# Three early experts, with their rows fetched ahead of the last routing, in an attention, FFN and mixture-of-experts kernel on Trainium2

## The chip, the cores and the metric

The kernel runs on one core of one Trainium2 chip, as one program and one launch. The metric is the device time of one execution in microseconds (us). The kernel before takes 1385.56 us, the median of three runs (1384.43 to 1387.48).

## The reference

Three stages, in float32. Attention: 4 batches of 8 heads, 576 positions of 64 values, where each query keeps its 32 best keys. FFN: 2304 tokens of 512 values, 2048 hidden values, squared ReLU. Then a mixture of experts, which the change concerns:

```python
logits = x @ w_gate
noise_scale = np.log1p(np.exp(x @ w_noise))
noisy_logits = logits + noise_scale * noise
top2 = np.argpartition(-noisy_logits, 2, axis=1)[:, :2]
...
for e in range(E):                      # 8 experts, 512 -> 1024 -> 512
    for k in range(2):
        mask = top2[:, k] == e
        h = np.maximum(x[mask] @ w1[e], 0.0)
        out[mask] += top2_w[mask, k, None] * (h @ w2[e])
```

## The kernel before, in words

Tokens go in 18 tiles of 128, in six chunks of three tiles (`CHUNKS`, L23). While attention works on later chunks, the FFN of finished ones runs as filler: `step` (L656) takes pieces from a list `background`, and, between them, pieces of the routing of a finished chunk (`route`, L177). The order in which each engine gets its instructions is made by a planner when the program is built: it goes by priority (mostly program order) and by a simulated time line; each engine then runs its list in order and waits on semaphores.

`route` turns the chunk's rows, computes the gates, counts how many tokens each expert has had so far (`base`) and scatters each token's row twice, by indirect DMA on POOL, into `xs` in DRAM, where every expert has its own slots (L259). The scatters are told to be independent of each other. A later read of `xs` waits for the scatters that stand ahead of it in program order.

`fetch(e, parts)` (L556) is a generator. For each tile of 128 slots it loads the rows from `xs` into `mr` (three buffers, issued on SyncE, L563), turns them with four TensorE transposes into a PSUM bank called `ph` (L566), writes a high and a low half into `xe` (ACT L570, DVE L571), and has POOL compute the gates into `info` (L548 to L554; `info` has two buffers). It yields after each tile, and at the end yields `xe` and `info`.

`expert(e, parts, ahead)` (L578) first gathers the present output rows into `cur` (POOL, L588), then makes 8 steps f. A step loads 512 KB of weights (`raww`, three buffers, L608), splits them into `wi` and `wo` (ACT L612, DVE L613; two buffers each), multiplies (`ph`, L619 to L621, two banks, 12 matmuls for each part), makes `ht` (ACT L625, DVE L626), and then does the second product of the step before (`second`, L596: `acc`, L600 to L602, three matmuls for each tile). From the second step on it advances the generator `ahead`, which fetches the next expert's rows. At the end DVE makes `y` (L640, three buffers) and POOL scatters it into `out` (L641). Slots are in two parts: 0 to 383 and 384 to 639 (`PARTS`, L77).

`EARLY` is 2: experts 0 and 1 work on the first part of their slots alone, behind the last FFN chunk and beside the last chunk's routing. So that the last chunk's tokens don't come into these slots, `ffn` raises `base` to 384 for the early experts (L313 to L316). When five of six chunks are routed, expert 0's rows are fetched (L827); expert 1's are fetched by expert 0 as `ahead`, and expert 1 waits with `once_routed` for the last routing before it fetches those of expert 2 (L831 to L840). Then come experts 2 to 7 with both parts, and then the second parts of experts 0 and 1, with their weights loaded again (`order`, L828; loop, L881).

`queued` (L166) stamps a matmul or transpose, and TensorE gets the stamped ones in program order. Stamped are all of the experts' matmuls, the transposes of `fetch`, and the TensorE work of the last routing; the FFN's are not.

Of the kernel before, what the change touches and what calls it, by code (L numbers as in the profile page):

```python
# [8 lines left out]
F32 = mybir.dt.float32  # L9
F32R = mybir.dt.float32r  # L10
# [7 lines left out]
P = 128  # L18
# [15 lines left out]
ROUTE_WAIT = 30  # L34
LAST_WAIT = 8
EXPERT_WAIT = 60
EARLY = 2
SOON = 300
FILL_LATER = 350
CONVERT_LATER = 200  # L40
# [15 lines left out]
def attention_ffn_moe(ctx: ExitStack, tc: tile.TileContext, q, k, v, w_ffn, w_route, noise, w_exp, out,  # L56
# [5 lines left out]
    NT, DM = out.shape  # L62
# [5 lines left out]
    NC = DM // P  # L68
# [8 lines left out]
    PARTS = [(0, 384), (384, CAP - 384)]  # L77
# [85 lines left out]
        nc.sync.dma_start(wsc[f][:, which], sp.bitcast(F32))  # L163


    def queued(inst):  # L166
        tc.stamp_issue_order_token(inst.ins, "experts")

    def evacuate(accs):
        xrs = []  # L170
# [104 lines left out]
    def ffn(t0, nt, xT):  # L275
# [37 lines left out]
        if t0 + nt == NTT:  # L313
            for e in range(EARLY):
                nc.vector.tensor_scalar(base[:, e:e + 1], base[:, e:e + 1], float(e * NT + PARTS[0][1]), None,
# [228 lines left out]
    def place(parts, t):  # L544
        return next((i, t * P - o) for i, (o, n) in enumerate(parts) if o <= t * P < o + n)

    def gate(gi, xr, e):
        nc.gpsimd.tensor_scalar(gi[:, 0:1], xr[:, DM + 2:DM + 3], float(e), xr[:, DM:DM + 1],  # L548
                                op0=ALU.is_equal, op1=ALU.mult)
        nc.gpsimd.tensor_scalar(gi[:, 1:2], xr[:, DM + 2:DM + 3], float(e), None, op0=ALU.is_equal)  # L550
        nc.gpsimd.tensor_scalar(gi[:, 1:2], gi[:, 1:2], -1.0, 1.0, op0=ALU.mult, op1=ALU.add)
        nc.gpsimd.tensor_tensor(gi[:, 1:2], gi[:, 1:2], xr[:, DM + 1:DM + 2], op=ALU.mult)
        nc.gpsimd.tensor_tensor(gi[:, 2:3], gi[:, 0:1], gi[:, 1:2], op=ALU.add)
        nc.gpsimd.tensor_copy(gi[:, 3:4].bitcast(I32), xr[:, DM + 3:DM + 4].bitcast(I32))  # L554

    def fetch(e, parts):  # L556

        xe = [mpool.tile([P, 2, NC, n], F32R, name=f"xe{o}") for o, n in parts]
        t0, t1 = parts[0][0] // P, sum(parts[-1]) // P
        info = mpool.tile([P, CAPT, 4], F32, name="info")  # L560
        for t in range(t0, t1):
            xr = mpool.tile([P, ROW], F32, name="mr", bufs=3)
            nc.sync.dma_start(xr, xs[e * NT + t * P:e * NT + (t + 1) * P, :])  # L563
            pt = ps_m.tile([P, DM], F32, name="ph")
            for c in range(NC):
                queued(nc.tensor.transpose(pt[:, c * P:(c + 1) * P], xr[:, c * P:(c + 1) * P], ident))  # L566
            i, off = place(parts, t)
            hi, lo = xe[i][:, 0, :, off:off + P], xe[i][:, 1, :, off:off + P]
            pv = pt.rearrange("p (c s) -> p c s", c=NC)
            nc.scalar.activation(hi, pv, AF.Copy)  # L570
            nc.vector.tensor_tensor(lo, pv, hi.bitcast(F32), op=ALU.subtract)  # L571
            gate(info[:, t, :], xr, e)
            yield None
        yield xe, info
# [3 lines left out]
    def expert(e, parts, ahead):  # L578
# [17 lines left out]
        def second(f, wo, hs):  # L596
            for t in tiles_:
                i, off = place(parts, t)
                sl = slice(off, off + P)
                queued(nc.tensor.matmul(acc[t], hs[i][:, 0, sl], wo[:, 0, :], start=(f == 0), stop=False))  # L600
                queued(nc.tensor.matmul(acc[t], hs[i][:, 0, sl], wo[:, 1, :], start=False, stop=False))  # L601
                queued(nc.tensor.matmul(acc[t], hs[i][:, 1, sl], wo[:, 0, :], start=False, stop=(f == NFE - 1)))  # L602
                yield True, 0.5
# [42 lines left out]
    found = []  # L646
# [9 lines left out]
    def step(n):  # L656

        state["due"] += n
        at = tc.cur_priority
        tc.cur_priority = at + FILL_LATER  # L660
        while state["due"] > 0 and (background or routing):
            cost = 1.0
            if routing and state["safe"] and routing[0][1] <= 0:
                try:
                    routing[0][1] = next(routing[0][0])
                    cost = 0.5
                except StopIteration:
                    routing.pop(0)
                    state["routed"] += 1
                    continue  # L670
            elif background:
                try:
                    state["safe"], cost = next(background[0][0])
                    background[0][1] -= cost
                except StopIteration:
                    state["safe"] = True
                    state["chunk"] += 1
                    background.pop(0)
                    continue
            state["due"] -= cost  # L680
            if routing:
                routing[0][1] -= cost
        if not background and not routing:
            state["due"] = 0.0
        tc.cur_priority = at
# [36 lines left out]
    for b in range(1, B):  # L722
        last = max(n for n, u in enumerate(units) if u[0] == b - 1)
# [97 lines left out]
    mpool = wctx.enter_context(tc.tile_pool(name="mpool", bufs=2))  # L821
    ps_m = wctx.enter_context(tc.tile_pool(name="ps_m", bufs=2, space=PSUM))
    after.append(ps_m)
    step(EXPERT_WAIT)
    while state["routed"] < len(chunks) - 1:
        step(1)
    found.append(list(fetch(0, PARTS[:1]))[-1])  # L827
    order = [(e, PARTS) for e in range(EARLY, E)] + [(e, PARTS[1:]) for e in range(EARLY)]  # L828
    last = fetch(*order[0])

    def once_routed(rows):  # L831
        while state["routed"] < len(chunks):
            yield None
        yield None
        yield None
        yield from rows

    for e in range(EARLY):
        ahead = fetch(e + 1, PARTS[:1]) if e + 1 < EARLY else once_routed(last)
        background.append([expert(e, PARTS[:1], ahead), 0])  # L840
    step(10 ** 6)

# [35 lines left out]
    for x in last:  # L878
        if x is not None:
            found.append(x)  # L880
    for i, (e, parts) in enumerate(order):  # L881
        ahead = fetch(*order[i + 1]) if i + 1 < E else iter(())
        for _ in expert(e, parts, ahead):
            pass
# [80 lines left out]
def build(shapes):  # L965
    import concourse.bacc as bacc

    nc = bacc.Bacc("TRN2", target_bir_lowering=False, num_devices=1)
    args = []
    for name, (shape, dt) in shapes.items():  # L970
        ap = nc.dram_tensor(name, shape, dt, kind="ExternalInput").ap()
        args.append(ap.bitcast(U32) if dt == mybir.dt.uint64 else ap)
    args.append(nc.dram_tensor("out", (2304, 512), F32, kind="ExternalOutput").ap())
    B, H, S, _ = SHAPE
    n_rows = B * H * (S // P) + B * H // 2
    with tile.TileContext(nc, schedule_with_timeline_sim=True) as tc, \
            tc.tile_pool(name="kpool", bufs=1) as kpool:
        keep = kpool.tile([P, n_rows, 4], F32, name="keep")
        attention_ffn_moe(tc, *args, keep=keep)
    return nc  # L980
# [61 lines left out]
```

## Time and profile before

| | before |
|---|---|
| median of three runs | 1385.56 us |
| the profiled execution, its own time | 1387.6 us |
| its span, first to last instruction | 1385.9 us |
| TensorE (PE) busy | 1246.5 us, 90% |
| TensorE weight loads (PEld) busy | 1084.5 us, 78% |
| VectorE (DVE), ScalarE (ACT), GpSimd (POOL) busy | 63%, 61%, 56% |
| mean granted TensorE clock | 0.962 |
| moved by DMA | 257.45 MB, mean 186 GB/s |

Busy time is a share of the whole span, over stages with different limits. Attention ends at about 760 us, the last FFN chunk at 878, and from there to the end the experts run. A group's mean time of a matmul is longer than the distance from one to the next, as matmuls are pipelined: for the pace one reads the starts.

### The profile page before, as it was taken

What the parts mean: (1) busy time and instruction counts of PE and PEld (TensorE: products, weight loads), DVE (VectorE), ACT (ScalarE), POOL (GpSimd) and SP (SyncE); (2) the same over time, 40 slices, a digit from 0 to 9 for tenths busy, and PEclk for the clock granted to TensorE, in tenths of its full rate; (3) what the DMA queues carried; (4) which work ended last, traced back from release to release, by engine and by line L of the source; (5) the groups of instructions that cost most, each with busy time, mean ns of one, the idle gap of its engine ahead of it and who ended that gap; (6) DMA issues with size and microseconds to landing.
All of it is one profiled execution on the core that took longest, in us unless ns stands there. A gap on an engine that the chain in (4) does not pass through costs nothing.

```text
span 1385.9 us, 25688 instructions
## 1 busy us (share of the span) xinstructions
PE 1246.5 (90%) x7937; PEld 1084.5 (78%) x7937; DVE 877.1 (63%) x4514; ACT 851.7 (61%) x1837; POOL 773.2 (56%) x1239
## 2 busy tenths in 40 slices
PE   3666689889999999899999999969999999999997
PEld 2555578768887887788888888759988898888986
DVE  7999979897767888988797001335444434444354
ACT  6888788888788888978796334524333233232343
POOL 6868999867776767777575424424413315041132
PEclk9786699999999999999999999989999999999999
DMA  9996688724764455275325767446534434343344
GB/s 333 352 345 228 208 309 296 261 91 153 251 209 142 143 178 191 62 237 183 130 92 176 270 224 263 146 139 198 163 125 127 142 117 149 111 150 118 119 155 144
DMA packets 85235, 257.45 MB, mean 186 GB/s; under 512 B 10716, under 2 KB 10844, under 8 KB 85088
## 3 DMA queue, kind: packets, MB, share of 16 engines
q1 hardware_dynamic: 75808, 227.32, 49.6%
q0 software_dynamic: 9280, 28.40, 5.7%
q8 instruction: 65, 1.06, 0.3%
q14 instruction: 82, 0.67, 0.1%
HBM read 205.71 MB, written 52.06 MB: 186 GB/s over the span
## 4 chain that ended last, share of the span: by engine, by line
PE 39%; issue 23%; DMA 9%; POOL 9%; DVE 9%; ACT 7%; POOLq 0%; SPq 0%; ACTq 0%; DVEq 0%
PE pa L491 5%; PE acc L282 4%; PE acc L283 4%; PE ps L371 4%; PE acc L284 4%; PE pf L296 3%; PE pf L298 3%; PE pf L297 3%; PE pa L454 3%; DMA out<-y,info 3%; DVE w L388 2%; POOL cur L588 2%; DMA mr<-xs 2%; DMA raw<-in_ffn 2%; DVE m L384 2%
## 5 line engine op out<-in xcount | busy, mean ns | idle before, releaser
L384 DVE MAX8 m<-sb 128x8 f32<-128x115 f32 (+1 forms) x720 | 191.7, 266 | 69.4 <-ACT sb L373 64.3
L442 POOL TENSOR_TENSOR sb<-sb,w 128x576 f32<-128x576 f32 x144 | 205.7, 1430 | 45.7 <-ACT w L441 44.4
L641 POOL DMA_INDIRECT out<-y,info x40 | 46.0, 1150 | 269.8 <-DVE y L640 252.6
L388 DVE MATCH_REPLACE8 w<-m,sb 128x115 f32<-128x115 f32 (+1 forms) x720 | 188.0, 264 | 0.0
L371 PE MATMUL ps<-K,qt 128*128 128x288 f32 (+2 forms) x640 | 134.1, 339 | 47.4 <-ACT sb L373 27.1
L619 PE MATMUL ph<-xe,wi 128*128 128x384 f32 (+1 forms) x512 | 163.4, 319 | 8.8 <-DVE ht L626 8.8
L620 PE MATMUL ph<-xe,wi 128*128 128x384 f32 (+1 forms) x512 | 158.7, 310 | 0.0
L621 PE MATMUL ph<-xe,wi 128*128 128x384 f32 (+1 forms) x512 | 158.4, 309 | 0.1
L371 PEld LDWEIGHTS ps<-K,qt 128*128 128x128 f32 x640 | 106.5, 210 | 64.6 <-ACT sb L373 36.1
L625 ACT ACTIVATE ht<-ph 128x384 fp32r<-128x384 f32 (+1 forms) x128 | 55.9, 437 | 148.4 <-PE ph L621 141.8
L612 ACT ACTIVATE wo<-raww 128x512 fp32r<-128x512 f32 x80 | 50.4, 631 | 143.7 <-PE acc L602 143.7
L306 POOL TENSOR_TENSOR gt<-r,gt 128x384 fp32r<-128x384 f32 x96 | 97.8, 1020 | 69.0 <-ACT gt L305 53.4
L443 ACT ACTIVATE sb<-sb,keep 128x576 f32<-128x576 f32 x144 | 112.2, 779 | 27.6 <-POOL sb L442 26.6
L626 DVE SCALAR_TENSOR_TENSOR ht<-ph,ht 128x384 fp32r<-128x384 f32 (+1 forms) x128 | 62.7, 490 | 101.9 <-ACT ht L625 100.8
L602 PE MATMUL acc<-wo,ht 128*128 128x512 f32 x320 | 126.6, 396 | 0.1
L600 PE MATMUL acc<-wo,ht 128*128 128x512 f32 x320 | 126.7, 396 | 0.0
L601 PE MATMUL acc<-wo,ht 128*128 128x512 f32 x320 | 126.3, 395 | 0.0
L613 DVE TENSOR_TENSOR wo<-raww,wo 128x512 fp32r<-128x512 f32 x80 | 55.3, 691 | 111.6 <-ACT wo L612 111.5
L296 PE MATMUL pf<-xT,wi 128*128 128x384 f32 x320 | 111.8, 350 | 9.3 <-ACT r L302 4.4
L282 PE MATMUL acc<-wo,gt 128*128 128x512 f32 x288 | 113.4, 407 | 4.7 <-ACT t L480 2.3
L441 ACT ACTIVATE w<-sb,keep 128x576 f32<-128x576 f32 x144 | 111.4, 775 | 9.9 <-POOL keep L437 9.3
L412 DVE MAX8 m<-w 128x8 f32<-128x288 f32 x288 | 116.0, 444 | 0.1
(190 smaller groups left out, 3527.2 us busy)
## 6 DMA issues: line engine op xcount, KB each, us to landing
wi<-wsc SPq DMA_DIRECT2D x96, 512.0 KB
wo<-wsc SPq DMA_DIRECT2D x96, 512.0 KB
raww<-in_exp SPq DMA_DIRECT2D x80, 512.0 KB
raw<-in_ffn SPq DMA_DIRECT2D x32, 512.0 KB
wsc<-csp SPq DMA_DIRECT2D x32, 512.0 KB
xs<-xr SPq DMA_DIRECT2D x40, 258.0 KB
mr<-xs SPq DMA_DIRECT2D x40, 258.0 KB
qn<-in_q SPq DMA_DIRECT2D x40, 256.0 KB
```

The costliest lines, as they stand in the source:

```text
L282: nc.tensor.matmul(acc[tt], gt[:, 0, sl], wo[:, 0, :], start=(f == 0), stop=False)
L296: nc.tensor.matmul(ph[:, 0:n], wi[:, 0, sl], xT[:, 0, c, 0:n], start=(c == 0), stop=False)
L371: nc.tensor.matmul(ps[:, n, 0:w], st, kt[:, at:at + w], start=(i == 0), stop=(i == len(pairs) - 1))
L384: in_turn(nc.vector.max(parts[i][1], sb[:, parts[i][0]]))
L388: in_turn(nc.vector.match_replace(out=w[:, sl], in_to_replace=top, in_values=sb[:, sl], imm_value=NEG))
L442: nc.gpsimd.tensor_tensor(sb, sb, w, op=ALU.subtract)
L600: queued(nc.tensor.matmul(acc[t], hs[i][:, 0, sl], wo[:, 0, :], start=(f == 0), stop=False))
L601: queued(nc.tensor.matmul(acc[t], hs[i][:, 0, sl], wo[:, 1, :], start=False, stop=False))
L602: queued(nc.tensor.matmul(acc[t], hs[i][:, 1, sl], wo[:, 0, :], start=False, stop=(f == NFE - 1)))
L619: queued(nc.tensor.matmul(ph[:, 0:n], wi[:, 0, sl], xe[i][:, 0, c, :], start=(c == 0), stop=False))
L620: queued(nc.tensor.matmul(ph[:, 0:n], wi[:, 0, sl], xe[i][:, 1, c, :], start=False, stop=False))
L621: queued(nc.tensor.matmul(ph[:, 0:n], wi[:, 1, sl], xe[i][:, 0, c, :], start=False, stop=(c == NC - 1)))
```

## The change

`EARLY` goes from 2 to 3. All rows of the early experts are fetched before the list of background work gets them, and so ahead of the last routing's scatters in program order; `xe0` has three buffers then, and the early transposes use the PSUM banks `acc2` in place of `ph`. The last early expert alone waits with `once_routed`. The full experts are 3 to 7, and the second parts of experts 0, 1 and 2 come last. Ahead of that loop the stamping is switched off, so that TensorE's order there is the planner's.

```diff
-EARLY = 2
+EARLY = 3
...
+    strict = [True]
+
     def queued(inst):
-        tc.stamp_issue_order_token(inst.ins, "experts")
+        if strict[0]:
+            tc.stamp_issue_order_token(inst.ins, "experts")
...
     def fetch(e, parts):
 
-        xe = [mpool.tile([P, 2, NC, n], F32R, name=f"xe{o}") for o, n in parts]
+        xe = [mpool.tile([P, 2, NC, n], F32R, name=f"xe{o}", bufs=EARLY if o == 0 else 2) for o, n in parts]
+        early = e < EARLY and parts[0][0] == 0
...
-            pt = ps_m.tile([P, DM], F32, name="ph")
+            pt = ps_m.tile([P, DM], F32, name="acc2" if early else "ph")
...
-    found.append(list(fetch(0, PARTS[:1]))[-1])
+    for e in range(EARLY):
+        found.append(list(fetch(e, PARTS[:1]))[-1])
...
     for e in range(EARLY):
-        ahead = fetch(e + 1, PARTS[:1]) if e + 1 < EARLY else once_routed(last)
+        ahead = once_routed(last) if e + 1 == EARLY else iter(())
         background.append([expert(e, PARTS[:1], ahead), 0])
...
     for x in last:
         if x is not None:
             found.append(x)
+    strict[0] = False
     for i, (e, parts) in enumerate(order):
```

## Rows read from the trace of the kernel before

**Rows 1.** The page's 40 equal slices: PE busy and granted clock, in tenths.

```profile
PE   3666689889999999899999999969999999999997
...
PEclk9786699999999999999999999989999999999999
```

**Rows 2.** Windows: length, busy us (instructions) of PE, PEld, DVE, ACT, POOL; clock, DMA share, GB/s.

```profile
866.00:869.00 3.00, 2.09 (x14) 1.60 (x15) 1.32 (x2) 1.69 (x4) 2.24 (x7) 1.00 0.94 367
...
901.00:914.70 13.70, 0.26 (x2) 0.01 (x1) 2.02 (x17) 0.63 (x1) 5.92 (x7) 0.62 0.55 195
...
918.00:972.00 54.00, 54.00 (x279) 48.30 (x278) 28.82 (x49) 22.54 (x42) 13.97 (x36) 1.00 0.55 163
972.00:1328.00 356.00, 349.55 (x1976) 314.23 (x1976) 148.30 (x249) 110.36 (x219) 102.70 (x221) 1.00 0.41 129
1328.00:1378.00 50.00, 47.39 (x300) 41.79 (x298) 29.84 (x54) 23.23 (x47) 15.48 (x23) 1.00 0.56 187
```

**Rows 3.** Timeline of PE: start us, us, engine, line, [idle before <- what ended it].

```profile
879.04 0.66 PE L185 MATMUL pf<-ident,xr 128*128 128x128 f32 x4 [0.21 <-ACT xr L173]
...
891.50 0.60 PE L566 MATMUL ph<-ident,mr 128*128 128x128 f32 x4
...
893.18 0.34 PE L620 MATMUL ph<-xe,wi 128*128 128x384 f32 x1
...
914.72 1.08 PE L566 MATMUL ph<-ident,mr 128*128 128x128 f32 x4 [13.46 <-DMA mr<-xs]
...
917.85 0.34 PE L620 MATMUL ph<-xe,wi 128*128 128x384 f32 x1
```

**Rows 4.** Timeline of SyncE's queue, 869 to 912 us: issues of mr loads.

```profile
869.34 0.32 SPq L563 DMA_DIRECT2D mr<-xs  x1
...
874.29 0.32 SPq L563 DMA_DIRECT2D mr<-xs  x1
...
911.97 4.23 SPq L563 DMA_DIRECT2D mr<-xs  x4
```

**Rows 5.** The chain of waits in order of time: start us, us, what.

```profile
855.61 5.96 DMA xs<-xr,si
861.77 4.21 DMA mr<-xs
...
909.00 2.81 DMA xs<-xr,si
911.97 2.62 DMA mr<-xs
```

**Rows 6.** Timeline of POOL: expert 1's first gather of output rows.

```profile
945.28 1.06 POOL L588 DMA_INDIRECT cur<-out,info  x1 [5.52 <-DMA out<-y,info]
```

**Rows 7.** Waits of PE from 915 to 1386 us: total us, times, longest.

```profile
PE ph L619 <- DVE ht L626: 8.8, 7, 2.4
```

**Rows 8.** Timeline of DVE and PE at two changes of expert, 1033 and 1335 us.

```profile
1033.53 0.75 DVE L640 SCALAR_TENSOR_TENSOR y<-acc,info,cur 128x512 f32<-128x512 f32 x1 [2.10 <-DMA out<-y,info]
...
1034.79 0.44 PE L619 MATMUL ph<-xe,wi 128*128 128x384 f32 x1 [1.23 <-DVE ht L626]
...
1335.73 0.39 PE L619 MATMUL ph<-xe,wi 128*128 128x256 f32 x1 [2.37 <-DVE ht L626]
```

**Rows 9.** Timeline of ACT: ht of an early expert; ht and wi of 256-row experts.

```profile
918.92 0.49 ACT L625 ACTIVATE ht<-ph 128x384 fp32r<-128x384 f32 x1 [2.48 <-PE ph L621]
...
923.14 0.49 ACT L625 ACTIVATE ht<-ph 128x384 fp32r<-128x384 f32 x1 [1.48 <-PE ph L621]
...
1343.54 0.38 ACT L625 ACTIVATE ht<-ph 128x256 fp32r<-128x256 f32 x1 [0.78 <-PE ph L621]
...
1346.35 0.38 ACT L625 ACTIVATE ht<-ph 128x256 fp32r<-128x256 f32 x1 [0.78 <-PE ph L621]
...
1362.91 0.63 ACT L612 ACTIVATE wi<-raww 128x512 fp32r<-128x512 f32 x1 [0.82 <-DMA raww<-in_exp]
...
1372.50 0.63 ACT L612 ACTIVATE wi<-raww 128x512 fp32r<-128x512 f32 x1 [1.77 <-DMA raww<-in_exp]
```

## The prediction

> **What bounds the kernel now.** I read the page's slices first: TensorE (PE) is over 90% busy in most slices from the sixth on, and its granted clock is full there, with one dip to a tenth or two below in the slice that starts at 901 us [rows 1]. The windows by stage then show where PE is not the bound. In 918 to 972 us it is busy all the time, in 972 to 1328 it misses 6.45 us, in 1328 to 1378 another 2.61, but between 901 and 914.7 it works 0.26 us of 13.70 [rows 2]. So the experts' stage is bound by PE, and has one hole. The timeline of PE names its end: the transposes at 914.72 us waited 13.46 us for a DMA of mr, a tile of the slots xs [rows 3].
>
> Why that DMA is late is read from the SyncE queue (SP) and the chain. Of expert 1's three row tiles two are asked for at 869.34 and 874.29; the next mr load is issued only at 911.97 [rows 4]. Just before it, the last scatter of the last routing into xs has landed (909.00 + 2.81), and the load takes 2.62 us more [rows 5]. The third tile stands behind the routing in program order, so it waits for scatters whose rows it never reads; PE's order of experts' work is fixed, so expert 1's matmuls wait behind its transposes.
>
> **The change, part by part.** The sum is made against the profiled execution: 1387.6 us, of which 1385.9 are the span. It lies 2.04 us above the median of the three runs, 1385.56; I carry that over at the end.
>
> *The hole.* All rows of the early experts are now read from xs before the last routing is written down, so no early load waits for its scatter. Minus 13.46 us [rows 3]. Nothing else is late there: three early experts of 8 steps, each 4.22 us of PE (from one ht to the next, 923.14 - 918.92 [rows 9]), are 101 us of work from about 880 us on, and the routing's rows are in SBUF at 914.6 [rows 5]. Two experts would have covered it too (67 us), so the third adds no more cover.
>
> *The clock behind the hole.* After it PE runs at half clock for a while: from the first transposes to the eighth matmul 917.85 - 914.72 = 3.13 us, where the same sequence took 893.18 - 891.50 = 1.68 before the hole [rows 3]. Without the hole minus 1.45 us.
>
> *Rows ahead.* Nine tiles are transposed ahead of expert 0's first matmul instead of three. Their PE work is moved, not added. SP, mr's three buffers and POOL's gates pace them: the first three loads go out at 861.77, just after the fifth chunk's scatters have landed [rows 5], the fourth at 869.34 [rows 4], when the first buffer is free. With the same 7.57 us again the third round goes out at 876.9 and lands, after 4.21 us [rows 5], at 881.1. PE finds the routing's transposes at 879.04 today [rows 3], and in the fixed order these stand behind the nine tiles. The last FFN chunk's own matmuls have no place in that order and go on meanwhile. I take plus 2.0 us (881.1 - 879.04). Bounds: minus 0.8, if the loads come sooner and the transposes, which get the acc2 banks, no longer share ph with the FFN; plus 8, if the FFN's last weights are also held up. For DMA is at 0.94 and 367 GB/s in 866 to 869 [rows 2], six more tiles of 258 KB take 4.2 us at that rate, and on SP a load that waits for its buffer holds the FFN's wo load behind it; with the 2.0 and about as much again for its release that makes 8. I stay near the small end, since both the DMA queue and PE catch up in the experts' work that follows.
>
> *POOL.* The gates are as many as before. But info has two buffers, so the third expert's gates wait until expert 0 has written its output. Behind them on POOL stands expert 1's gather of cur, which waits for the same write anyway (at 945.28, 5.52 us [rows 6]); y needs it some 25 us later. No cost; without that cover some 4 us, as three tiles' gates together take less than four of the 1.06 us gathers of that row.
>
> *One 640-row expert fewer.* On 918 to 1386 PE waits seven times for ht, 8.8 us [rows 7]. At each of five changes between full experts it is 1.2 us: DVE holds y, which waits for the write of an earlier y, and ht is queued behind it [rows 8]. Expert 2 leaves this row: four changes are left, minus 1.23 us. The change to the first 256-row expert (2.37 us [rows 8]) stays. Changes between 384-row experts cost nothing: 918 to 972 holds one and has no idle time [rows 2]. The one more max on base lies on DVE, which is busy 28.82 of 54 us in the early experts [rows 2]: nothing.
>
> *One 256-row expert more.* Its matmuls are those that expert 2 had before, but its weights are loaded and split a second time: 8 x 512 KB, 16 ACT and 16 DVE instructions. In the 256-row experts this matters: PE needs 2.81 us a step (1346.35 - 1343.54), while the wi conversions of the last four steps come (1372.50 - 1362.91) / 3 = 3.20 us apart [rows 9]. In the kernel before the lead of the conversions runs out only at the end. Eight more steps at the weights' pace: 8 x 0.39 = plus 3.1 us. Bounds: 0, if the conversions are put in an order that keeps the lead, and 5.5, if another change of 2.37 us comes with it. I take 3.1, as the row that it rests on is of the same shape.
>
> *The free order.* PE's order is no longer written down for the full experts and the last three. In steps within an expert there is nothing to win, since PE has no idle time there. The stalls that are left (8.8 - 1.23 = 7.6 us) are waits of f = 1 for a ph bank that DVE frees late; no other matmul is ready then. I take 0, between minus 7.6 and, as an order by a plan can be wrong on the chip, plus several us (below).
>
> **Sum:** - 13.46 - 1.45 - 1.23 + 3.1 + 2.0 = - 11.0 us: 1376.6 for the profiled execution, 1374.5 on the scale of the median. The bounds without the free order are - 16.9 and - 2.6: 1368.6 and 1382.9.
>
> A row against a rule: in 866 to 869 twelve transposes ran with over a microsecond of idle time between and the granted clock stayed 1.00, the 2.4 GHz level [rows 2]; the row gives the nine tiles no price in clock. The Trainium skill, TensorE: Matmul & The Clock Gate, Part 4: PE-mode transpose, says that the full clock doesn't come on for transposes. It speaks against this change, which gathers 36 of them in one stretch; by it the sum would hold another 7.3 us, as the third rival works out from rows.
>
> **Rivals.**
> 1. *The free order also fills the stalls.* The seven waits of rows 7 go but for the one counted: 1374.5 - 7.6 = 1367 us. For it: the planner sees all matmuls of the next step. Against it: they need the same bank. 0.12.
> 2. *The wait moves to the front.* The nine tiles come slower than I think, PE stands about as long at 870 to 890 as it now does at 901. The hole is paid there, up to 13.46, less what the FFN fills: 1383 to 1387. For it: DMA is full in this stretch [rows 2], and the order is fixed. Against it: the third round needs only two more of the distances seen. 0.10.
> 3. *The clock falls in the fetch.* PE drops to the 1.2 GHz level among the 36 transposes and stays there until the FFN ends: some 8.5 us of FFN matmuls (12.4 us from 866 to 878.4, less transposes, idle time and expert 0's first matmuls) then take 3.13 / 1.68 = 1.86 times as long [rows 3]: plus 7.3, 1381.8. Against it: twelve transposes in 3 us left the clock at 1.00 [rows 2]. 0.03.
> 4. *Slower: a bad free order.* If PE is given a step's second product right behind its first, each step waits for its own ht, about 1.23 us (the wait of rows 8 for the same release). In the 24 steps of the 256-row experts that is 29.5 us: 1404. It decides from 11.0 / 1.23 = 9 such steps on; of 64 in all. Against it: a first product is earlier in the program and normally ready first. For it: weights that come late by the plan change who is ready, in the last experts above all. 0.09.
> 5. *It doesn't do what it says:* some early load still stands behind the scatter, the hole stays, with 3.1 us for the third expert less 1.23: 1387. The new loop takes all early rows before the routing's step, so 0.03.
>
> **How the numbers follow.** The forecast has 0.63, rivals 1 to 5 hold 0.12, 0.10, 0.03, 0.09, 0.03. The forecast's own range, 1368.6 to 1382.9, is widened downwards for half of the first rival and upwards for most of the second: 1365 to 1385; outside lie the fourth, the fifth and edges, about 0.2. A measurement of this kernel can tell about 0.2%, 2.8 us, from no change: faster means below 1382.8. That takes the forecast, the first and the third, and a little of the second: 0.79. Same: most of the second and half of the fifth, 0.11. Slower: 0.10.
>
> **What would show it.** Right: no PE wait over 2 us for mr between 901 and 915 us, granted clock 1.00 throughout the slices of the experts; mr loads in three rounds at about 862, 869 and 877; routing's transposes on PE some 2 us later than 879; raww loaded 88 times instead of 80, four changes of 1.2 us; about 3 us of PE waits for wi or raww in the last two 256-row experts. Wrong: a wait of PE for mr of 8 us or more ahead of expert 0; PE waits for ht within an expert's steps; PE stalls in the last 75 us beyond 6 us; or a PE that shows more busy time in the experts than before.

## The result: 1370.84 us, 1.1% faster, and the profile after

The changed kernel takes 1370.84 us in the median (1369.23 to 1376.11, four runs), the kernel before beside it 1386.52: 15.7 us less, ratio 0.9891 (95% interval 0.9867 to 0.9915). Five more runs on another chip gave 0.9886 (0.9866 to 0.9907). The forecast was 1374.5 us, 11.0 us less.

In the profile of after the lines of `route`, `ffn` and attention are 3 higher, those of `fetch` and `expert` 4: the FFN's last product is L287, the transposes of `fetch` L570, the gates L551 to L557, the experts' matmuls L604 to L606 and L623 to L625, ht L629 and L630, y L644.

The page of after, its slices of PE and of the granted clock (compare [rows 1]):

```profile
PE   3666689789999999899999999899999999999997
...
PEclk9878699999999999999999999999999999999999
```

The dip at 901 us is gone. The windows of after, columns as in [rows 2], with the FFN's end and the routing split more finely:

```profile
860.00:880.00 20.00, 15.20 (x78) 12.10 (x77) 6.31 (x10) 9.79 (x20) 13.06 (x44) 0.96 0.86 287
880.00:901.00 21.00, 18.70 (x100) 15.33 (x101) 7.08 (x23) 10.16 (x21) 2.73 (x12) 0.87 0.11 30
901.00:914.70 13.70, 13.70 (x77) 12.23 (x76) 8.37 (x33) 6.03 (x12) 8.69 (x18) 1.00 0.54 171
...
1004.00:1290.00 286.00, 286.00 (x1629) 258.22 (x1628) 123.61 (x207) 93.07 (x184) 85.66 (x181) 1.00 0.42 133
1290.00:1360.00 70.00, 65.86 (x413) 57.53 (x411) 41.80 (x76) 33.06 (x67) 18.35 (x35) 1.00 0.57 186
```

The stretch in which PE stood now has 13.70 of 13.70 us busy. The full experts have no idle time at all, where [rows 2] has 6.45 us. Against that, 860 to 901 lost time, and the clock there is under 1.00: a new loss ahead of expert 0. PE's timeline of after shows it:

```profile
862.00 0.39 PE L287 MATMUL acc<-wo,gt 128*128 128x512 f32 x1
...
874.12 1.04 PE L570 MATMUL acc<-ident,mr 128*128 128x128 f32 x8
878.13 1.79 PE L570 MATMUL acc<-ident,mr 128*128 128x128 f32 x8 [2.97 <-DMA mr<-xs]
880.30 1.11 PE L570 MATMUL acc<-ident,mr 128*128 128x128 f32 x4 [0.37 <-DVE xe L575]
882.46 1.09 PE L570 MATMUL acc<-ident,mr 128*128 128x128 f32 x4 [1.05 <-DMA mr<-xs]
883.20 0.67 PE L623 MATMUL ph<-xe,wi 128*128 128x384 f32 x1
```

After the FFN's last product at 873.4 PE has nothing but transposes for 9 us, in an order that lets nothing pass, and waits for their rows. Eight transposes take 1.79 us in place of 1.04, and the first matmul of expert 0 takes 0.67 us: behind the wait of 2.97 us the granted clock is 0.59 from 878.1 to 880.3 us and 0.50, the 1.2 GHz level, from there to 885.27.

The PE waits of after in the last experts (columns as in [rows 7]); none is for ht:

```profile
PE ph L623 <- ACT wi L616: 1.5, 1, 1.5
PE acc L604 <- DVE y L644: 0.8, 1, 0.8
PE ph L623 <- DVE xe L575: 0.6, 1, 0.6
PE ph L625 <- DVE wi L617: 0.4, 2, 0.2
```

**Where the time went.** The two profiled executions differ by 18.4 us of span (1385.9 and 1367.5). Not all of it is the change. The last matmul that both have in the same place of PE's order is the L287 at 862.00 above; in the kernel before it is this row of PE's timeline:

```profile
865.34 0.39 PE L284 MATMUL acc<-wo,gt 128*128 128x512 f32 x1
```

So 3.3 us were there before the first experts' instruction; 15.1 us remain, which agrees with the medians' 15.7. (PE's order up to this matmul is the same in every kernel of this document. So the time from its start to the start of PE's last matmul, called *from the shared matmul* below, compares two profiles without what differs ahead of it: 512.4 us before and 496.9 after, 15.5 less.) The 15.1 us are made of the hole, - 13.46 (with nothing in its place), and all waits for ht, - 8.8; against these, idle time from 840 to 901 us, where PE was idle 8.5 us in the windows of after (1.37 + 4.80 + 2.30) and 5.0 before, + 3.4; and in the last experts 3.3 us of waits, + 3.3. The slow clock moved: from 878 us to 885 it costs 2.5 us (0.75 on the first eight transposes, 0.5 on the next four, and 2.81 us in place of 1.5 from 882.46 to 885.27), where it cost 1.45 behind the hole: + 1.1. Together - 14.5; the last 0.6 us have no row. This sum counts PE's time. The transposes at 882.46 waited for their rows, so a full clock ahead of them would only have lengthened that wait: of the 2.5 us only the last 1.3 lie on the path.

### The profile page after: what moved, and what is told of

Its sections match the earlier page's. It is cut to its first block, busy times and chain, and to the rows that moved or that the text cites. A ratio compares the mean times of both kernels' runs of the same rounds, so it can differ in the third digit from the quotient of the medians.

```text
span 1367.5 us, 25764 instructions
## 1 busy us (share of the span) xinstructions
PE 1242.3 (91%) x7937; PEld 1082.6 (79%) x7937; DVE 891.6 (65%) x4531; ACT 861.8 (63%) x1853; POOL 772.3 (56%) x1239
## 4 chain that ended last, share of the span: by engine, by line
PE 53%; DVE 12%; issue 10%; DMA 9%; ACT 6%; POOL 5%; POOLq 0%; SPq 0%; ACTq 0%; DVEq 0%
PE pa L494 4%; PE acc L285 4%; PE acc L286 4%; PE ps L374 4%; PE acc L287 3%; PE pf L299 3%; PE pf L300 3%; PE pf L301 3%; PE ph L623 3%; PE ph L625 3%; PE ph L624 3%; PE acc L604 3%; PE pa L457 3%; PE acc L605 3%; DVE w L391 3%
## 5 line engine op out<-in xcount | busy, mean ns | idle before, releaser
L629 ACT ACTIVATE ht<-ph 128x384 fp32r<-128x384 f32 (+1 forms) x128 | 55.9, 437 | 194.4 <-PE ph L625 194.3
L630 DVE SCALAR_TENSOR_TENSOR ht<-ph,ht 128x384 fp32r<-128x384 f32 (+1 forms) x128 | 62.6, 489 | 165.2 <-ACT ht L629 165.0
L623 PE MATMUL ph<-xe,wi 128*128 128x256 f32 (+1 forms) x512 | 160.1, 313 | 2.2 <-ACT wi L616 1.5
L625 PE MATMUL ph<-xe,wi 128*128 128x256 f32 (+1 forms) x512 | 158.7, 310 | 0.4 <-DVE wi L617 0.4
L624 PE MATMUL ph<-xe,wi 128*128 128x256 f32 (+1 forms) x512 | 158.9, 310 | 0.0
L604 PE MATMUL acc<-wo,ht 128*128 128x512 f32 x320 | 125.8, 397 | 0.8 <-DVE y L644 0.8
L605 PE MATMUL acc<-wo,ht 128*128 128x512 f32 x320 | 125.1, 394 | 0.0
L299 PE MATMUL pf<-xT,wi 128*128 128x384 f32 x320 | 111.7, 349 | 10.0 <-DMA wi<-wsc 3.5
L285 PE MATMUL acc<-wo,gt 128*128 128x512 f32 x288 | 113.8, 409 | 6.3 <-DMA wo<-wsc 3.8
L444 ACT ACTIVATE w<-sb,keep 128x576 f32<-128x576 f32 x144 | 111.4, 775 | 11.9 <-POOL keep L440 11.2
L457 PE MATMUL pa<-ident,sb 128*128 128x128 f32 x576 | 96.6, 293 | 19.0 <-ACT sb L446 10.2
L300 PE MATMUL pf<-xT,wi 128*128 128x384 f32 x320 | 110.0, 344 | 3.6 <-POOL xT L472 3.6
L286 PE MATMUL acc<-wo,gt 128*128 128x512 f32 x288 | 110.7, 398 | 0.0
```

Source lines behind the costliest of these rows:

```text
L285: nc.tensor.matmul(acc[tt], gt[:, 0, sl], wo[:, 0, :], start=(f == 0), stop=False)
L286: nc.tensor.matmul(acc[tt], gt[:, 0, sl], wo[:, 1, :], start=False, stop=False)
L299: nc.tensor.matmul(ph[:, 0:n], wi[:, 0, sl], xT[:, 0, c, 0:n], start=(c == 0), stop=False)
L623: queued(nc.tensor.matmul(ph[:, 0:n], wi[:, 0, sl], xe[i][:, 0, c, :], start=(c == 0), stop=False))
L624: queued(nc.tensor.matmul(ph[:, 0:n], wi[:, 0, sl], xe[i][:, 1, c, :], start=False, stop=False))
L625: queued(nc.tensor.matmul(ph[:, 0:n], wi[:, 1, sl], xe[i][:, 0, c, :], start=False, stop=(c == NC - 1)))
```

## The experiments

Each kernel ran five rounds beside the kernel before; ratios are to that.

**The two parts alone.** The diff holds two parts that can be set one without the other: rows ahead, and the free order. Each was put into the kernel before by itself, with two early experts.

```diff
 # e3_free_alone: the kernel before
+    strict = [True]
...
-        tc.stamp_issue_order_token(inst.ins, "experts")
+        if strict[0]:
+            tc.stamp_issue_order_token(inst.ins, "experts")
...
+    strict[0] = False
     for i, (e, parts) in enumerate(order):
```

> The kernel before with nothing but the order set free after its two early experts. Theory: the hole of 13.5 us stays, the seven waits for ht (8.8 us) go: about 1378 us, 8 us under the kernel before. Rival: the free order gains only in the company of the other parts, within 2 us of the kernel before, 1385 to 1388 us.

Measured: 1377.87 us, ratio 0.9934 (0.9917 to 0.9952), 10.1 us under its kernel before. Waits of PE from 840 us on:

```profile
PE ph L569 <- DMA mr<-xs: 14.3, 2, 13.5
...
PE ph L622 <- DVE ht L629: 1.3, 1, 1.3
```

The hole is whole; of the waits for ht 1.3 us are left, 7.5 fewer than before. From the shared matmul it is 504.7 us, 7.8 under the kernel before. So the free order is worth what these waits cost, by itself.

```diff
 # e6_ahead_alone: the changed kernel
-EARLY = 3
+EARLY = 2
...
-    strict[0] = False
```

> The kernel before with nothing but all rows of its two early experts ahead of the last routing (TensorE's order fixed to the end, two early experts). Theory: this part takes out the hole and the slow clock behind it and nothing else, 13.5 + 1.5 us, less up to 1 us of waits for the fourth to sixth tile: 14 to 15 us under the kernel before, about 1373 us, with the seven waits for ht (about 9 us) still there. Rival: the rows ahead also cost at the front what they cost with three experts (6 us): 8 to 9 us under, about 1379 us.

Measured: 1373.26 us, ratio 0.9884 (0.9865 to 0.9903), 15.0 us under. Waits of PE from 862 us on:

```profile
PE ph L623 <- DVE ht L630: 9.0, 6, 2.2
PE acc L285 <- DMA wo<-wsc: 2.5, 2, 1.3
...
PE acc L570 <- DMA mr<-xs: 0.5, 1, 0.5
```

The rows ahead remove the hole and the slow clock behind it, and leave the waits for ht (498.2 us from the shared matmul, 14.3 under). Two parts, 1.16% and 0.66%: together 1.8%, more than the 1.1% that the whole change gave.

**The third expert.**

```diff
 # e2_two_ahead: the changed kernel
-EARLY = 3
+EARLY = 2
```

> The changed kernel with two early experts, all their rows ahead, order free after them. Theory: the third expert gives no cover that is needed; without it three tiles less are fetched ahead (the PE wait of 2.97 us, or the one of 1.05, goes, 1 to 3 us) and 8 steps of weights less are loaded (about 3 us of waits in the last experts go): 4 to 6 us under the changed kernel, about 1366 us, and no wait of PE over 2 us at the routing. Rival: two experts are done before the routing's rows are there, and the hole comes back behind them: over 1375 us, with a PE wait for mr of several us near 945 us.

Measured: 1360.82 us, ratio 0.9812 (0.9798 to 0.9826). Both parts' 1.8% are there whole (1.9% measured), and the third expert costs 10 us (0.9891 against 0.9812, intervals apart; 9.8 us from the shared matmul, 496.9 against 487.1), twice what I expected. PE's waits from 840 us on:

```profile
PE acc L570 <- DMA mr<-xs: 1.5, 2, 1.1
PE acc L285 <- DMA wo<-wsc: 1.5, 1, 1.5
...
PE ph L625 <- DVE wi L617: 0.4, 2, 0.2
```

No wait near 945 us, where the rival put one: PE is busy all of 915 to 1280 us. Two experts cover the routing.

**The fixed order with three experts.**

```diff
 # e1_fixed_order: the changed kernel
-    strict[0] = False
```

> The changed kernel with TensorE's order written down to the end, as before. Theory: it is the free order that took the waits for ht away (8.8 us in the kernel before, none after), so they come back: four changes of 1.2 us between full experts and some 2.4 us at the first 256-row expert, with a second such change perhaps; 7 to 9 us over the changed kernel, about 1379 us. Rival: they went because xe0 has a third buffer and the early rows no longer use ph, so that DVE's and ACT's order came out otherwise; then the fixed order costs under 2 us, 1371 to 1372 us.

Measured: 1379.79 us, ratio 0.9944 (0.9927 to 0.9962). The waits for ht are back, and with them the loss:

```profile
PE ph L623 <- DVE ht L630: 7.3, 5, 1.8
PE acc L570 <- DMA mr<-xs: 3.6, 2, 3.3
```

So it was the order. How it fills these waits is seen in the changed kernel's PE timeline at the change from expert 3 to 4:

```profile
1048.43 0.28 PE L625 MATMUL ph<-xe,wi 128*128 128x256 f32 x1
1048.54 0.39 PE L606 MATMUL acc<-wo,ht 128*128 128x512 f32 x1
...
1051.34 0.34 PE L623 MATMUL ph<-xe,wi 128*128 128x384 f32 x1
...
1052.91 0.39 PE L604 MATMUL acc<-wo,ht 128*128 128x512 f32 x1
...
1054.31 0.34 PE L623 MATMUL ph<-xe,wi 128*128 128x384 f32 x1
```

In the fixed order both parts' first products (384 and 256 columns) stand together, and the second products behind both. The planner takes them apart: second products stand between the two parts (from 1048.54 on) and six of them (1052.91 to 1054.31) inside the 384-column product. They need no ph bank, so the six alone give DVE 1.4 us more to free one.

**The buffers of mr.** SyncE's queue in the changed kernel, with the loads of the nine tiles, and POOL ahead of the second round:

```profile
859.74 1.49 SPq L567 DMA_DIRECT2D mr<-xs  x3
...
870.23 0.80 SPq L567 DMA_DIRECT2D mr<-xs  x2
...
873.49 3.18 SPq L567 DMA_DIRECT2D mr<-xs  x3
...
879.14 0.32 SPq L567 DMA_DIRECT2D mr<-xs  x1
```

```profile
865.17 0.33 POOL L551 TENSOR_SCALAR info<-mr 128x1 f32<-128x1 f32 x1 [1.01 <-DMA mr<-xs]
...
866.73 1.15 POOL L592 DMA_INDIRECT cur<-out,info  x1 [0.15 <-POOL info L554]
...
868.85 1.11 POOL L592 DMA_INDIRECT cur<-out,info  x1 [0.17 <-POOL info L557]
870.00 0.35 POOL L555 TENSOR_TENSOR info<-info,mr 128x1 f32<-128x1 f32 x2
```

The first two tiles are in SBUF by 865.8 and turned by 868.3, but the next loads go out at 870.23 only: the buffers' last reader, a gate (L555), stands on POOL behind two gathers of cur.

```diff
 # e4_six_mr: the changed kernel
-            xr = mpool.tile([P, ROW], F32, name="mr", bufs=3)
+            xr = mpool.tile([P, ROW], F32, name="mr", bufs=6)
```

> The changed kernel with six buffers for mr instead of three. Theory: the three buffers and the gates that free them pace the nine tiles; with six the second round is asked for at once, the PE waits for mr of 2.97 and 1.05 us go and the clock holds: 3 to 6 us under the changed kernel, about 1366 us. Rival: DMA is full then (0.86 of it in 860 to 880 us), the tiles or the FFN's weights come as late as before: within 1.5 us of the changed kernel, about 1371 us, with the waits moved to wi or wo of the FFN.

Measured: 1363.30 us, ratio 0.9831 (0.9807 to 0.9854), some 8 us under the changed kernel (8.1 from the shared matmul). Six loads go out at once, and of the waits for mr 0.7 us are left:

```profile
862.23 2.70 SPq L567 DMA_DIRECT2D mr<-xs  x6
```

```profile
PE acc L570 <- DVE xe L575: 2.7, 2, 1.7
...
PE acc L570 <- DMA mr<-xs: 0.7, 1, 0.7
```

The rival's shift to the FFN's weights did not come, but PE waits for the conversion of the rows (xe) instead, so that all its waits from 840 us to expert 0 and the routing fall only from 8.3 to 6.4 us. The last experts gained too: there PE waits 1.5 us in place of 3.3, and none of it for wi. With 3.4 us at the lower clock (881.3 to 884.7) in place of 6.8, the rows hold some 5 of the 8 us.

**The buffers of raww.** In the last experts of after the longest wait begins on SyncE: a weight load stands behind an mr load, which waits 6.2 us for its buffer.

```profile
1294.30 0.33 SPq L612 DMA_DIRECT2D raww<-in_exp  x1
1300.58 0.33 SPq L567 DMA_DIRECT2D mr<-xs  x1
1301.00 0.38 SPq L612 DMA_DIRECT2D raww<-in_exp  x1
```

Its weights reach ACT at 1305.0, where ACT has then been idle 4.63 us, and PE waits 1.54.

```diff
 # e5_raww4: the changed kernel
-            raw = mpool.tile([P, 2, DM], F32, name="raww", bufs=3)
+            raw = mpool.tile([P, 2, DM], F32, name="raww", bufs=4)
```

> The changed kernel with four raww buffers instead of three. Theory of the prediction: in the last three experts PE falls to the pace of the weights, as a raww buffer comes free too late; with a fourth the 2 to 3 us of PE waits there go, about 1368 us. Rival: the longest of these waits (1.54 us) comes from SyncE's queue, where a weight load stands behind an mr load that waits for its buffer; a fourth raww buffer gives then less than 1.5 us or nothing, 1369 to 1372 us.

Measured: 1371.28 us, ratio 0.9872 (0.9853 to 0.9891), a gain over the changed kernel that the intervals can't tell from none. The profile says more: from 1290 us to its end PE has no wait with a row at all, so with a fourth buffer all 3.3 us go, more than either theory gave it, and from the shared matmul it is 2.9 us shorter. But ahead of expert 0 this execution waited longer, among others

```profile
PE acc L570 <- DMA mr<-xs: 4.6, 2, 3.3
PE ph L299 <- DMA wi<-wsc: 3.4, 2, 1.9
```

**Both sets of buffers.** e9 has the two edits above together, with three early experts; e8 the same with two, e7 two with six mr alone. The changed kernel ran again beside e8 and e9.

> The changed kernel once more, as it is, beside the two below on the same chip. Every theory expects what it took before, 1370 to 1372 us, 0.989 of the kernel before; its waits at the fetch and in the last experts in the same places.

Measured: 1373.56 us, ratio 0.9886 (0.9866 to 0.9907): 1.6 us over the expectation, with the ratio and the places of the waits as expected.

> The changed kernel with six mr and four raww buffers. Theory: what the third early expert costs (some 10 us against two experts) is waits for these buffers alone, for its matmuls are those it would have had anyway; with both sets of buffers it comes to where two experts are, 1360 to 1362 us, with under 1 us of PE waits in the last 75 us. Rival: some of it is its second load of weights, its further changes of expert or the three tiles' own time in front; then 2 to 5 us stay, 1363 to 1366 us.

Measured: 1361.86 us, ratio 0.9821 (0.9793 to 0.9849). The windows of this kernel:

```profile
860.00:880.00 20.00, 17.01 (x92) 14.05 (x90) 6.50 (x10) 12.10 (x23) 13.54 (x44) 1.00 0.92 310
880.00:900.00 20.00, 18.62 (x110) 15.39 (x111) 8.15 (x27) 10.99 (x22) 3.45 (x15) 1.00 0.20 60
...
1280.00:1350.00 70.00, 70.00 (x452) 62.71 (x450) 47.63 (x81) 36.80 (x73) 24.65 (x39) 1.00 0.62 197
```

PE has no idle time in the last 70 us of its work, and the clock is full at the front. From the shared matmul it is 485.0 us, 11.9 under the changed kernel and 2.1 under two experts (e2). So what a third expert costs is waits for these two sets of buffers; its second load of weights is then hidden. The times agree, though their interval alone would also allow the rival's 2 us.

> Two early experts, rows ahead, free order, and six mr buffers. Theory: with six tiles the three buffers cost only 1 to 1.5 us (a PE wait for mr of 1.1 us before expert 0), so this is 1 to 2 us under the same kernel with three buffers, about 1359 us. Rival: nothing is left to gain there, the FFN's last weights and the routing's own chain set the front: within 0.7 us of it, about 1361 us.

Measured: 1361.93 us, ratio 0.9809 (0.9783 to 0.9836): the rival, nothing left to gain. A load of the FFN's wo goes out behind the six on SyncE's queue, at 863.65, and takes 6.30 us to land; PE waits 2.62 us for it, and from the end of that wait on the clock is at its lower level among the FFN's own matmuls (the second line is a window, columns as in [rows 2]).

```profile
870.08 0.76 PE L285 MATMUL acc<-wo,gt 128*128 128x512 f32 x1 [2.62 <-DMA wo<-wsc]
...
869.50:876.20 6.70, 6.12 (x19) 4.97 (x20) 1.88 (x3) 1.32 (x3) 6.06 (x23) 0.50 0.44 148
```

> Two early experts, rows ahead, free order, six mr and four raww buffers. Theory: the waits that are left in the last two experts with three raww buffers are 1 to 2 us, and the front gains little: 1359 to 1361 us, 0.980 to 0.981 of the kernel before, the best of all or level with two experts alone. Rival: another order by the planner brings waits elsewhere, 1362 us or more.

Measured: 1365.06 us, ratio 0.9828 (0.9808 to 0.9848). The time is the rival's, and there is a wait at the front and another at the end, in PE's and in DVE's timeline:

```profile
872.22 0.77 PE L285 MATMUL acc<-wo,gt 128*128 128x512 f32 x1 [3.66 <-DMA wo<-wsc]
...
1313.74 0.75 DVE L644 SCALAR_TENSOR_TENSOR y<-acc,info,cur 128x512 f32<-128x512 f32 x1 [1.77 <-DMA out<-y,info]
...
1314.87 0.39 PE L623 MATMUL ph<-xe,wi 128*128 128x256 f32 x1 [1.35 <-DVE ht L630]
```

But the rival's cause isn't shown. PE's order up to about 1340 us is the same as in e7, which has the first wait too, 2.62 us long. At the second place DVE has y ahead of ht in e7 as well, but there y didn't wait for the write of an earlier y:

```profile
1309.37 0.75 DVE L644 SCALAR_TENSOR_TENSOR y<-acc,info,cur 128x512 f32<-128x512 f32 x1
```

So both are DMAs that landed later in an order that e7 has too; why they did isn't settled.

The lowest median is that of two early experts with rows ahead and the free order, 1360.82 us; three with more buffers and two with six mr lie within its interval, so the runs don't tell which of the three is best.

**Open.** One kernel fetches the third expert's rows later, by expert 1:

```diff
 # e10_third_later: the changed kernel
-    for e in range(EARLY):
+    for e in range(2):
         found.append(list(fetch(e, PARTS[:1]))[-1])
...
-        ahead = once_routed(last) if e + 1 == EARLY else iter(())
+        ahead = (iter(()), fetch(2, PARTS[:1]), once_routed(last))[e]
```

> The changed kernel, but only experts 0 and 1 have their rows ahead; the third early expert's rows are fetched by expert 1, behind the last routing. Theory: some 6 us of what the third expert costs are the seventh to ninth tile in front of expert 0 (PE waits for mr, slow clock); these go, and the waits in the last experts (3 us) stay: about 1365 us. Rival: the third expert costs by its second load of weights and its changes, wherever its rows are fetched: within 2 us of the changed kernel, 1369 to 1373 us.

Measured: 1366.24 us, ratio 0.9832 (0.9811 to 0.9852), the theory's time. But its profiled execution, at 1370.19 us the longest of the five, waits at the front as the changed kernel does, for the sixth tile:

```profile
PE acc L570 <- DMA mr<-xs: 3.9, 1, 3.9
```

Fewer tiles don't rule the wait out, and from the shared matmul this execution is 495.1 us, 1.8 under the changed kernel. How much of the wait comes in which execution isn't settled: the five runs spread from 1361.88 to 1370.19. So the theory's cause isn't shown for this kernel.

## Why the prediction was right, and where it was not

The direction and the range held, and so did the mechanism of the hole. One term was wrong by more than all others, the free order, and it was on the good side. That the time came within 4 us of the forecast is in part luck: 7.6 us of unforeseen gain stand against some 4 us of unforeseen loss.

- *The hole*, - 13.46: right. No wait for mr is left between 901 and 915 us, and the part alone (e6) gave 15.0 us, hole and clock.
- *Cover*: right that two experts would do; e2 shows it.
- *The clock*, - 1.45: wrong in the sum. The slow stretch behind the hole went, but another came at the front, 2.5 us of PE's time. In the changed kernel it began behind a wait of 2.97 us, with eight transposes just ahead of it. The transposes alone don't explain it: in e9 36 of them run at a clock of 1.00, the first 20 among the FFN's matmuls and the last 16 with nothing between them from 877.50 to 881.46 us but waits of 1.66 and 0.23. The Trainium skill, TensorE: Matmul & The Clock Gate, Part 4: PE-mode transpose, says that the full clock doesn't come on for them; the rows of e9 don't agree with it. Nor is it settled by e9: e4 has the same order of PE there, waits of 1.66 and 0.65, and the clock fell at 881.3. The third rival's mechanism, a lower clock among the FFN's matmuls, is not seen in the changed kernel, where the FFN was done, but it is in e7 and e8, with waits of 2.62 and 3.66 us. (The row that I held against it, 866 to 869, has 0.78 us of idle time between the transposes and 0.39 ahead of them, not over a microsecond between.)
- *Rows ahead*, + 2.0: the mechanism was right, the size was short. The fourth load went out 10.5 us behind the first (870.23 - 859.74) where I had 7.57, the ninth at 879.14 (I had 876.9 for the round), and expert 0 started at 883.20; + 3.4 us idle. I took the round time of [rows 4] as a given; it is the place of the gates behind the gathers on POOL, and this order was made anew.
- *POOL and info*: right. The third expert's gates waited for expert 0's write until 932.8, the gathers behind them began at 935.3, and no PE wait follows.
- *The free order*, 0: the step that failed. I wrote of the ht waits that "no other matmul is ready then". That holds for the fixed order, where all second products of the step before are behind or already spent. A free order can have kept them back, and did. The first rival was right, in full: 8.8 us of waits went instead of the 1.23 that I gave to one change fewer; e3 and e1 show that it was the order.
- *One 256-row expert more*, + 3.1: the number came out, 3.3 us of waits in the last experts, but the path didn't, and that is luck. The steady pace of 3.20 us a step did not set PE's pace. Of the 3.3 us only 1.9 are waits for weights, 1.54 of them from one load held up on SyncE's queue; the other 1.4 are waits for y and xe at changes of expert, to which the term gave nothing. That a fourth buffer would remove it all (e5) the prediction did not say.
- *Slower by a bad free order* (rival 4): no sign of it in any kernel with the order free; the waits for ht in a profile come to 1.65 us at most (e8).

By its own terms the sum was - 11.0; the free order adds - 7.6, the front and its clock + 1.4 and + 2.6, the last experts + 0.2: - 14.4, against 15.1 in the profiles.

## What to carry to other kernels

A load that waits for scatters which it doesn't need is cured by its place in the program; ask how much cover is needed before adding more, as every further tile held ahead wants buffers. Where an order is fixed by hand and PE waits for a bank, look for work of an earlier step that needs no bank: the fixed order may have spent it too soon. A buffer's release is as late as the place of its last reader in that engine's queue, here a gate of 0.2 us behind two gathers of 1.1.

## What the runs showed of the hardware that was not expected

Between the two executions of before and after, 3.3 us of difference stood ahead of the first changed instruction of PE, and the five runs of one kernel on one chip spread by up to 9.6 us (1358.32 to 1367.89 in e4). Two profiles of the changed kernel (after and e11) differ by 0.9 us ahead of the shared matmul and by 1.3 behind it. One profile against another therefore says where time went, and by the stretch from the shared matmul what it was worth to 1 or 2 us; for the whole time the ratios do.

The granted clock can fall in one execution and not in another behind almost the same work: in e4 and e9 PE has the same order and the same wait of 1.66 us at 879 to 880 us; in e4, where the next wait was 0.65 us, the clock was 0.50 from 881.3 to 884.7, and in e9, where it was 0.23, it stayed 1.00.
